# Gated attention and mixer block on one core: second-product tiles begin in any free strip, hand-over pause 0.51, first raw tokens loaded before their row statistics

## The chip, the cores and the metric

The kernel runs on one core of a Trainium2 chip. The core has a matrix engine (PE, with its weight loads as PEld), a vector engine (DVE), a scalar engine (ACT), GpSimd (POOL) and a queue engine (SP), each with an instruction queue of its own. They meet through semaphores. The metric is the time of one execution in device microseconds. Before the change it was 1044.77 us, the median of three runs between 1043.12 and 1045.74.

## What is computed

One input x of 2048 tokens by 448 features goes through two branches, and a gate per token mixes them. All operands are float32; the matrix products are made from high and low parts, three products for one.

```python
def reference(A_x, A_wqkv, A_wo, B_x, B_w1, B_b1, B_w2, B_b2, gate_w):
    x = A_x
    g = sigmoid((x * gate_w).sum(-1, keepdims=True))
    # A: 16 heads of 28: softmax(q k^T / sqrt(28)) v, then wo
    a = attention(x, A_wqkv, A_wo)
    # B: layernorm over features, 448 -> 1792, GELU (tanh form), 1792 -> 448
    y = (x - mean) / sqrt(var + 1e-5)
    b = gelu(y @ B_w1 + B_b1) @ B_w2 + B_b2
    return g * a + (1 - g) * b
```

## The kernel before

The work has two stages. In the **strip stage** the array is used as four strips of 32 rows. Each strip works off matmuls of its own, and four run side by side. A tile of output (128 x 512 or 128 x 448, in one of six PSUM banks, the buffer `bk`) needs a visit to each of the four strips; the kernel makes these one after the other, since all four add into the same bank. The tiles come in this order: queries and keys (`QK`, 25 tiles here, after three made with the whole array), values (`Val`, 16), then for each chunk c of 512 tokens 14 tiles of the first MLP product (`Up`, operands `w1f` and `yh`/`yl`) and 4 tiles of the second (`Down`, operands `w2h`/`w2l` and `hh`/`hl`). An Up, QK or Val tile takes 42 matmuls in its four visits, a Down tile 168, since its sum runs over all 14 hidden tiles. Up has 512 columns, Val and Down 448 or 450.

Beside them the strips make **row maxima** (line 212 on PE, line 214 on DVE): for each head the maximum over the keys of a 128 x 512 block of scores, needed by the softmax later. There are 1024 of them; 578 stand in the strip stage, and the rest in the attention stage, one or two in a turn (`lone`).

In the **attention stage** a loop of 257 turns makes scores (line 1139), exponentials on ACT (line 1145) and the products with the values (line 1183). An agenda puts DMAs and GpSimd work at given turns. In the last of the four head groups it also fetches the MLP result (`fetch_acc`, line 982), weighs it on GpSimd (`weigh_acc`, lines 986 and 987), and projects with wo (lines 1001 to 1003).

What sets the order: `Strips.run` is a planner that runs while the program is built. It holds a time for each strip, DVE, ACT, POOL and the DMAs, takes the strip that is free first, and gives it a matmul of a tile whose operands are ready by its own count. Otherwise it moves that strip on by 0.1. Its figures are numbers in the code: 0.232 for a matmul of 512 columns, 0.204 for one of Down, `HOP` for the pause between the end of a visit and the begin of the tile's next visit in another strip, and some for each helper. The result is a fixed order for every queue. At a hand-over, SP waits for the last matmul of a visit and raises the semaphore `hand` (line 529); the first matmul of the next visit waits for it (line 487).

A Down tile i begins in strip i and goes round from there (`next`, line 378). Its products stand in a fixed order: high parts of the hidden tile by both parts of w2 for f = 0 to 13, then the low parts. `lacks` (line 389) asks for the next product in that order only.

The layer norm: `want_stats` reads x and makes means and variances on DVE; `rows` turns them into two rows, stored to DRAM (line 142). `want_ln(c)` loads these rows for chunk c to all partitions (`lnr`, line 160) and the raw tokens of the chunk (`raw`, four tiles), subtracts the mean (line 679 on GpSimd for c > 1, line 686 on DVE otherwise), multiplies (line 691, GpSimd) and splits into `yh` (ACT, line 707) and `yl` (GpSimd, line 708). All of chunk c must be split before its first Up product.

Of the kernel before, what the change touches and what calls it, by code (L numbers as in the profile page):

```python
# [35 lines left out]
def kernel(ctx: ExitStack, tc: tile.TileContext, xt, wqk, wv, wo, xk, w1, b1, w2, b2,  # L36
# [204 lines left out]
    HOP = 0.6  # L241
# [5 lines left out]
    hh, hl = [], []  # L247
    mhp = []

    class Piece:  # L250
# [10 lines left out]
        def lacks(self, st, m, now):  # L261
            return False

# [105 lines left out]
    class Down(Piece):  # L369
# [3 lines left out]
        fixed = True  # L373

# [3 lines left out]
        def next(self, s):  # L378
            return s == (self.i + 4 - len(self.rem)) % 4
# [9 lines left out]
        def lacks(self, st, m, now):  # L389
            f, p = (m // 2, 0) if m < 2 * NF else (m - 2 * NF, 1)  # L390
            return st.hready.get((self.c, f, p), 1e9) > now or self.c == 0 and st.w2ready.get(f, 1e9) > now
# [12 lines left out]
    class Strips:  # L404
# [44 lines left out]
        def pick(self, s, now, over=None):  # L449
            for x in self.live:  # L450
                if x.bar(self):
                    continue
                if x.next(s) and not x.busy and x.ready <= now and (over is None or isinstance(x, Up) and x.c == over.c):
                    return x
            if over is None and self.tiles and self.tiles[0].next(s) and self.tiles[0].start(self, now):
                b = min(self.free, key=lambda b: self.free[b], default=None)
                if b is not None and self.free[b] <= now:
                    x = self.tiles.pop(0)
                    x.bank = b
                    del self.free[b]  # L460
                    self.live.append(x)
                    started(self, x, now)
                    return x
            return None

        def run(self):
            while self.tiles or self.live:
# [12 lines left out]
                if v is None or v[0].lacks(self, v[2], now):  # L480
                    self.t[s] = now + 0.1
                    continue
                x, ops, m = v
                a, b = ops[m] if not x.fixed else (ops[m][0][ops[m][2]][ops[m][3], ops[m][4]], ops[m][1][ops[m][2]][ops[m][3]])
# [173 lines left out]
    def rows(st):  # L658
        ln_std()
        st.use("dve", st.clock, 0.15)  # L660
        st.use("act", st.dve + 0.2, 2.2)

        def second():
            ln_rows()
            st.use("dve", st.clock, 0.6)
            st.at(st.dve + 0.2, ln_store)
            st.at(st.dve + 3.5, lambda: want_ln(st, 0))
            for f in range(NW, NF):
                st.at(st.dve + 3.6, lambda f=f: want_w1(st, f, kept=True))
            st.at(st.dve + 3.7, st.feed.pump)  # L670

        st.at(st.act + 0.2, second)

    def want_ln(st, c):
        cs = slice(c * CH, (c + 1) * CH)

        def use(t, r, late=False):
            if c > 1:
                nc.gpsimd.tensor_sub(r, r, lnr[c][:, 0])
                st.use("pool", st.clock, 1.35)  # L680
                scale(t, r)
                return
            if c == 0 and not late:
                st.at(st.clock + 1.5, lambda: use(t, r, True))
# [12 lines left out]
        for t in range(4):  # L697
            st.feed.add(xt[t, :, cs], 256, lambda r, t=t: use(t, r), kept=True,
                        first=(lambda: ln_rows_load(c)) if t == 0 else None)
# [88 lines left out]
    def schedule_head(st):  # L788
# [4 lines left out]
        st.late, st.later = False, []  # L793
# [8 lines left out]
        for f in range(NW):  # L802
            want_w1(st, f, after=54.0)
# [272 lines left out]
    def begun(n, turn):  # L1076

        g, c = divmod(n, NC)
        if n + 1 < NG * NC:
# [3 lines left out]
            at(turn + 10, lambda: load_ms(n + 1))  # L1083
# [7 lines left out]
        if g == NG - 1:  # L1091
            for i in range(TPC):
                at(turn + 8 + i, lambda i=i: fetch_acc(c, i))
                at(turn + 10 + i // 2, lambda i=i: weigh_acc(c, i))
# [3 lines left out]
    def valued(n, turn):  # L1098
# [9 lines left out]
        if g == NG - 1:  # L1108
            for i in range(TPC):
                tail.append((turn + 8 + i, c * TPC + i))  # L1110
# [153 lines left out]
```

## Time and profile before

| | us |
|---|---|
| runs | 1043.12, 1044.77, 1045.74 |
| profiled execution, own time | 1043.61 |
| its span (first to last instruction) | 1041.8 |
| before the strips (loads, first three QK tiles) | 0 to 16.6 |
| strip stage, first to last matmul of line 488 | 16.6 to 447.9 |
| attention stage, to the end of PE's work | 447.9 to 1036.6 |
| last DVE work, last stores, end of program | 1036.6 to 1041.8 |
| granted clock, mean | 0.999 |

The page's share of busy time counts PE as busy when any strip works. Four strips that are each busy, and one that is busy while three wait, look the same in it. How full the strips are is read from the number of matmuls that a stretch of time holds. A stretch also counts the ones that were already running when it began, so the short ones count some more per microsecond than the long ones, and a stretch is compared with a full one of the same kind and length.

### The profile page before, as it was taken

The page shows a single profiled execution, that of the slowest core. Times are in us where ns is not written, and L with a number is a line of the kernel's source. Part 1 is how long each engine was busy: PE and PEld are TensorE (multiplying, and loading weights), DVE is VectorE, ACT ScalarE, POOL GpSimd, SP SyncE. Part 2 cuts the span into 40 slices and gives each one's busy share as a digit, 9 for nine tenths or more (in the row PEclk, how much of TensorE's full clock was granted, in tenths as well). Part 3 has the DMA queues.
Part 4 walks back from the last instruction along what each step waited for, and adds up shares of the span by engine and source line. Part 5 has one row for each costly group of instructions (what it writes and reads, how often), then busy time and mean ns, then how long its engine had stood idle before and what let it go on. Part 6 is the DMA issues. An engine that isn't in the chain of part 4 may idle for free.

```text
span 1041.8 us, 30993 instructions
## 1 busy us (share of the span) xinstructions
PE 1033.5 (99%) x13170; PEld 683.0 (66%) x13170; DVE 748.6 (72%) x1182; ACT 663.3 (64%) x1016; POOL 369.1 (35%) x392
## 2 busy tenths in 40 slices
PE   9999999999999999999999999999999999999998
PEld 6999999999999999954444444444444444454455
DVE  4899898999999999966666666466666666634101
ACT  5334365044034034079999999999999999957763
POOL 5566468526325026651111011220111224463451
PEclk9999999999999999999999999999999999999999
DMA  7686533221210012350010101320002202111121
GB/s 242 208 257 217 205 110 98 72 66 30 61 38 12 7 43 55 82 155 23 14 26 22 30 5 40 82 60 13 20 21 65 53 12 57 30 64 48 53 66 45
DMA packets 47787, 73.20 MB, mean 70 GB/s; under 512 B 13840, under 2 KB 28816, under 8 KB 46848
## 3 DMA queue, kind: packets, MB, share of 16 engines
q1 hardware_dynamic: 33888, 39.11, 13.4%
q0 software_dynamic: 5120, 16.89, 5.8%
q10 hardware_dynamic: 8640, 15.21, 4.0%
q8 instruction: 103, 1.69, 0.7%
q14 instruction: 36, 0.29, 0.1%
HBM read 51.75 MB, written 19.31 MB: 68 GB/s over the span
## 4 chain that ended last, share of the span: by engine, by line
PE 99%; DMA 0%; DVE 0%; SPq 0%; issue 0%; ACT 0%
PE bk L488 37%; PE bk L1183 25%; PE bk L1139 17%; PE bk L212 15%; PE bk L1001 2%; PE bk L1003 1%; PE bk L1002 1%; PE bk L920 1%; DMA first<-in_xt 0%; PE bk L945 0%; PE bk L1066 0%; SPq L898 0%; PE bk L1060 0%; DVE xl L106 0%; DVE ob L1023 0%
## 5 line engine op out<-in xcount | busy, mean ns | idle before, releaser
L214 DVE TENSOR_REDUCE mx<-bk 128x1 f32<-128x512 f32 x1024 | 683.3, 689 | 185.0 <-PE bk L212 163.0
L1145 ACT ACTIVATE p<-bk 128x1024 f32<-128x1024 f32 x743 | 510.6, 760 | 64.5 <-PE bk L1139 39.4
L212 PE MATMUL bk<-kd,qd 28*128 28x512 f32 x1024 | 439.6, 430 | 0.0
L212 PEld LDWEIGHTS bk<-kd,qd 28*128 28x128 f32 x1024 | 186.1, 182 | 198.0 <-DVE mx L214 173.8
L488 PE MATMUL bk<-yh,w1f 32*128 32x512 f32 x1568 | 191.5, 393 | 0.0
L488 PE MATMUL bk<-yl,w1f 32*128 32x512 f32 x784 | 166.7, 392 | 0.0
L488 PEld LDWEIGHTS bk<-yh,w1f 32*128 32x128 f32 x1568 | 154.9, 183 | 1.2 <-ACT h L355 0.2
L488 PE MATMUL bk<-w2h,hh 32*128 32x448 f32 x896 | 145.3, 367 | 0.0
L488 PE MATMUL bk<-w2l,hh 32*128 32x448 f32 x896 | 144.2, 363 | 0.0
L1041 POOL TENSOR_TENSOR ot<-ob,rc 128x512 f32<-128x512 f32 x12 | 15.4, 1284 | 346.3 <-DMA rc<-rls 226.6
L1183 PE MATMUL bk<-p,vb 128*32 128x512 f32 x1024 | 136.6, 605 | 0.1
L1183 PE MATMUL bk<-p,va 128*32 128x512 f32 x1024 | 136.4, 605 | 0.0
L363 POOL TENSOR_TENSOR hl<-h,hh 128x512 fp32r<-128x512 f32 x56 | 72.5, 1308 | 132.9 <-ACT hh L356 106.7
L488 PEld LDWEIGHTS bk<-yl,w1f 32*128 32x128 f32 x784 | 106.0, 183 | 0.1
L488 PEld LDWEIGHTS bk<-w2h,hh 32*128 32x128 f32 x896 | 103.5, 183 | 0.4
L488 PEld LDWEIGHTS bk<-w2l,hh 32*128 32x128 f32 x896 | 103.5, 183 | 0.2
L488 PE MATMUL bk<-w2h,hl 32*128 32x448 f32 x896 | 93.1, 362 | 0.0
L1139 PE MATMUL bk<-yh,ka 29*128 29x512 f32 x512 | 92.5, 470 | 0.0
L1139 PE MATMUL bk<-yh,kb 29*128 29x512 f32 x512 | 87.6, 477 | 0.0
L398 ACT ACTIVATE gb<-bk 128x448 f32<-128x448 f32 x8 | 4.4, 545 | 129.4 <-PE bk L488 129.4
L355 ACT ACTIVATE h<-bk,b1s 128x512 f32<-128x512 f32 x56 | 38.3, 684 | 73.6 <-PE bk L488 67.4
L488 PEld LDWEIGHTS bk<-w2h,hl 32*128 32x128 f32 x896 | 82.1, 183 | 0.3
(141 smaller groups left out, 1637.2 us busy)
## 6 DMA issues: line engine op xcount, KB each, us to landing
qk<-qo ACTq DMA_DIRECT2D x28, 256.0 KB
raw<-in_xt SPq DMA_DIRECT2D x17, 256.0 KB
vs<-vt ACTq DMA_DIRECT2D x16, 256.0 KB
rc<-rls SPq DMA_DIRECT2D x60, 64.0 KB
bxr<-in_xk POOLq DMA_DIRECT2D x8, 448.0 KB, 6.3
acc<-gbs SPq DMA_DIRECT2D x16, 224.0 KB
out_y<-acc SPq DMA_DIRECT2D x16, 224.0 KB
qd<-qk SPq DMA_DIRECT2D x60, 56.0 KB
```

The lines of the kernel that those rows point to most:

```text
L212: nc.tensor.matmul(ps, self.qd[n % 2][r, i * P:(i + 1) * P], self.kd[r, k * 512:(k + 1) * 512], start=True, stop=True)
L214: nc.vector.reduce_max(self.mx[n % 2][:, j, i, k:k + 1], ps, axis=AX)
L355: nc.scalar.activation(h, bk[:, self.bank], AF.Gelu_apprx_tanh, bias=b1s[:, f:f + 1])
L363: nc.gpsimd.tensor_sub(hl[f], h, hh[f].bitcast(F32))
L488: mm = nc.tensor.matmul(bk[:, x.bank, :n], a, b, start=x.first, stop=(len(x.rem) == 1 and m == len(ops) - 1), skip_group_check=True)
L920: nc.tensor.matmul(bk[:, b], w, v, start=(i == 0), stop=(i == len(ops) - 1), skip_group_check=True)
L1001: nc.tensor.matmul(po, h, woh[:, g], start=(g == 0), stop=False, skip_group_check=True)
L1002: nc.tensor.matmul(po, h, wol[:, g], start=False, stop=False, skip_group_check=True)
L1041: nc.gpsimd.tensor_mul(ot[g][:, c * CH:(c + 1) * CH], ob, rc)
L1139: nc.tensor.matmul(bk[:, b], w[r, ks], q[r], start=(p == 0), stop=(p == 2), skip_group_check=True)
L1145: nc.scalar.activation(t[:, i:e], bk[:, b + i:b + e], AF.Exp, scale=SCALE)
L1183: nc.tensor.matmul(bk[32 * j:32 * j + 32, 7], vg[n // NC][:, k, 32 * j:32 * j + 32], prob[4 * b + j], start=(k == 0), stop=(k == NT - 1), ...
```

## The change

It touches six things.

1. `HOP` falls from 0.6 to 0.51. It moves instructions in the planner's order; no wait is taken out of the program.
2. A Down tile begins in any strip in which no other Down tile of its chunk began (`begun_in`), and goes round from there.
3. In a visit the planner takes the next product whose operands are ready, and not the next in the fixed order (the list is rearranged with `ops.insert(m, ops.pop(k))`). So low parts can come ahead of high parts. The sum is the same up to the order of additions.
4. The raw tokens of chunk 0 are asked for when the statistics are done, and the `lnr` load stands apart in `shift_rows`; the subtractions are held until the planner expects `lnr`. The first ten w1 tiles are asked for from 60 and not from 54 of the planner's time.
5. For chunk 1 the subtraction goes from DVE to GpSimd, as it did for chunks 2 and 3.
6. In the attention stage `load_ms` goes from turn + 10 to turn + 13, `fetch_acc` and `weigh_acc` move by 4 turns, the projections of chunk 1 move by 4 turns, `lone` prefers the strip with the most row maxima until the least has 192, and a strip's newly loaded keys count as there 2 turns sooner.

```diff
-    HOP = 0.6
+    HOP = 0.51
...
+    begun_in = set()
...
-        def lacks(self, st, m, now):
+        def lacks(self, st, op, now):
             return False
+
+        def begin(self, s):
+            pass
...
+        first_strip = None
...
         def next(self, s):
-            return s == (self.i + 4 - len(self.rem)) % 4
+            if self.first_strip is None:
+                return (self.c, s) not in begun_in
+            return s == (self.first_strip + 4 - len(self.rem)) % 4
+
+        def begin(self, s):
+            if self.first_strip is None:
+                self.first_strip = s
+                begun_in.add((self.c, s))
...
-        def lacks(self, st, m, now):
-            f, p = (m // 2, 0) if m < 2 * NF else (m - 2 * NF, 1)
+        def lacks(self, st, op, now):
+            f, p = op[2], int(op[0] is hl)
...
-                if v is None or v[0].lacks(self, v[2], now):
+                k = next((k for k in range(v[2], len(v[1])) if not v[0].lacks(self, v[1][k], now)), None) if v else None
+                if k is None:
                     self.t[s] = now + 0.1
                     continue
                 x, ops, m = v
+                ops.insert(m, ops.pop(k))
...
-            st.at(st.dve + 3.5, lambda: want_ln(st, 0))
+            st.at(st.dve + 3.5, shift_rows)
...
+        def shift_rows():
+            ln_rows_load(0)
+            st.use("pool", st.clock, 0.8)
+            st.shifted = st.get(st.pool, 512) + 0.7
+            for go in st.unshifted:
+                st.at(st.shifted, go)
+
         st.at(st.act + 0.2, second)
+        st.at(st.clock + 0.1, lambda: want_ln(st, 0))
...
-            if c > 1:
+            if c > 0:
                 nc.gpsimd.tensor_sub(r, r, lnr[c][:, 0])
...
-                st.at(st.clock + 1.5, lambda: use(t, r, True))
+                def go():
+                    use(t, r, True)
+
+                if st.shifted is None:
+                    st.unshifted.append(go)
+                else:
+                    st.at(max(st.clock, st.shifted), go)
...
-            want_w1(st, f, after=54.0)
+            want_w1(st, f, after=60.0)
...
-            at(turn + 10, lambda: load_ms(n + 1))
+            at(turn + 13, lambda: load_ms(n + 1))
...
-                at(turn + 8 + i, lambda i=i: fetch_acc(c, i))
-                at(turn + 10 + i // 2, lambda i=i: weigh_acc(c, i))
+                at(turn + 12 + i, lambda i=i: fetch_acc(c, i))
+                at(turn + 14 + i // 2, lambda i=i: weigh_acc(c, i))
...
-                tail.append((turn + 8 + i, c * TPC + i))
+                tail.append((turn + (12 if c == 1 else 8) + i, c * TPC + i))
...
-        s = min((s for s in strips if rowmax.ready(s) and turn >= cold[s]), key=lambda s: rowmax.cnt[s], default=None)
+        s = min((s for s in strips if rowmax.ready(s) and turn >= cold[s]), key=lambda s: rowmax.cnt[s] * (1 if min(rowmax.cnt) > 192 else -1), default=None)
...
-                cold[j] = turn + 7
+                cold[j] = turn + 5
```

Three places show what the planner makes of it. The numbers behind names are the program's own buffer numbers.

**GpSimd, at the end of the w1 splits of the strip stage**, before: the last w1 split, the load of the statistics rows, the four loads of raw tokens (`raw<-in_xt`), and the first multiplication and split of chunk 0.

```order
L97 TENSOR_TENSOR w1f9_2081<-raw0_130,w1f9_2081 64x128
L160 DMA lnr_2248<-lns_89 128x2x512
L571 DMA raw1_131<-in_xt 128x512
L571 DMA raw2_132<-in_xt 128x512
L571 DMA raw3_133<-in_xt 128x512
L571 DMA raw0_130<-in_xt 128x512
L691 TENSOR_TENSOR raw1_131<-raw1_131,lnr_2248 128x512
L708 TENSOR_TENSOR yl_111<-raw1_131,yh_110 128x512
```

The same place with the change:

```order
L160 DMA lnr_2008<-lns_89 128x2x512
L96 TENSOR_TENSOR w1f6_1934<-first1_135,w1f6_1934 128x384
L97 TENSOR_TENSOR w1f6_1934<-first1_135,w1f6_1934 64x128
L586 DMA raw2_132<-in_xt 128x512
L96 TENSOR_TENSOR w1f7_1964<-first2_136,w1f7_1964 128x384
L97 TENSOR_TENSOR w1f7_1964<-first2_136,w1f7_1964 64x128
L586 DMA raw3_133<-in_xt 128x512
L96 TENSOR_TENSOR w1f8_2106<-first3_137,w1f8_2106 128x384
L97 TENSOR_TENSOR w1f8_2106<-first3_137,w1f8_2106 64x128
L96 TENSOR_TENSOR w1f9_2140<-raw0_130,w1f9_2140 128x384
L97 TENSOR_TENSOR w1f9_2140<-raw0_130,w1f9_2140 64x128
L720 TENSOR_TENSOR raw1_131<-raw1_131,lnr_2008 128x512
```

The first raw load stands three rows ahead of this piece, and the fourth in the row right behind it. So three of the four now stand among the w1 splits, the first of them ahead of `lnr`; the fourth waits for its buffer `raw0`, which holds w1 tile 9 until that is split.

**PE, at the border of the Up and Down tiles of chunk 0**, before: `hh13` is the last hidden tile's high part, and `hl` are low parts.

```order
L488 MATMUL bk_115<-w2h13_3789,hh13_2923 128x448 x3
L488 MATMUL bk_115<-w2h5_3391,hh5_2915 128x448
L488 MATMUL bk_115<-w2l13_3790,hh13_2923 128x448 x2
L488 MATMUL bk_115<-w2l5_3392,hh5_2915 128x448
L488 MATMUL bk_115<-w2l13_3790,hh13_2923 128x448
L488 MATMUL bk_115<-w2h0_3143,hl0_2924 128x448 x2
L488 MATMUL bk_115<-w2h6_3486,hh6_2916 128x448
L488 MATMUL bk_115<-w2h0_3143,hl0_2924 128x448
L488 MATMUL bk_115<-w2h1_3180,hl1_2925 128x448 x2
L488 MATMUL bk_115<-w2l6_3487,hh6_2916 128x448
```

The same border with the change:

```order
L503 MATMUL bk_115<-yh_110,w1f13_3003 128x512
L503 MATMUL bk_115<-w2l9_3601,hh9_2943 128x448
L503 MATMUL bk_115<-w2l10_3709,hh10_2944 128x448
L503 MATMUL bk_115<-w2h7_3534,hh7_2941 128x448
L503 MATMUL bk_115<-w2h10_3708,hh10_2944 128x448
L503 MATMUL bk_115<-w2h6_3509,hh6_2940 128x448
L503 MATMUL bk_115<-w2h0_3171,hl0_2948 128x448
L503 MATMUL bk_115<-w2l7_3535,hh7_2941 128x448
L503 MATMUL bk_115<-w2l10_3709,hh10_2944 128x448
L503 MATMUL bk_115<-w2l6_3510,hh6_2940 128x448
L503 MATMUL bk_115<-w2h1_3213,hl1_2949 128x448
```

Before, no low part stands ahead of the last high part of its tile. Now the low parts `hl0` and `hl1` stand among high parts 6 to 10, and so ahead of `hh11` to `hh13` of their own tile.

**SP, at the end of the program**, before: the result of the MLP comes in by `acc<-gbs` (line 982), the output goes out by `out_y<-acc` (line 1009). These are the last rows.

```order
L1035 DMA rc_16365<-rls_92 32x512 x4
L982 DMA acc_16481<-gbs_90 128x448
L1009 DMA out_y<-acc_16065 128x448
L982 DMA acc_16519<-gbs_90 128x448
L1009 DMA out_y<-acc_16104 128x448
L982 DMA acc_16559<-gbs_90 128x448
L1009 DMA out_y<-acc_16145 128x448
L982 DMA acc_16597<-gbs_90 128x448
L1009 DMA out_y<-acc_16183 128x448
L1009 DMA out_y<-acc_16481 128x448
```

With the change (lines 1011 and 1038):

```order
L1064 DMA rc_16367<-rls_92 32x512 x4
L1038 DMA out_y<-acc_16150 128x448
L1038 DMA out_y<-acc_16187 128x448
L1038 DMA out_y<-acc_16227 128x448
L1038 DMA out_y<-acc_16265 128x448
L1011 DMA acc_16621<-gbs_90 128x448
L1011 DMA acc_16643<-gbs_90 128x448
L1011 DMA acc_16669<-gbs_90 128x448
L1011 DMA acc_16693<-gbs_90 128x448
L1038 DMA out_y<-acc_16621 128x448
```

The last four loads of the MLP result stood one by one between the stores of the chunk ahead. Now all four stand behind the last of these stores.

The number of row maxima in the strip stage, counted in the order as built, is 569 and was 578. The number of attention turns stays 257.

More of the change, by code (lines that the diff above doesn't have):

```diff
@@ L459, in pick @@
                     x.bank = b
+                    x.begin(s)
                     del self.free[b]
@@ L698, in want_ln @@
             st.feed.add(xt[t, :, cs], 256, lambda r, t=t: use(t, r), kept=True,
-                        first=(lambda: ln_rows_load(c)) if t == 0 else None)
+                        first=(lambda: ln_rows_load(c)) if t == 0 and c else None)
         st.feed.pump()
@@ L792, in schedule_head @@
         st.wready.update({0: 0.0, 3: 0.0, 4: 0.0})
-        st.late, st.later = False, []
+        st.late, st.later, st.shifted, st.unshifted = False, [], None, []
         st.xs, st.wvn, st.stats, st.lns, st.go, st.yn = {}, 0, 0, {}, {0}, {}
```

## The prediction

> **What bounds the kernel now.** I read the page first, then windows of the strip stage, then the waits.
>
> ```profile
> PE 1033.5 (99%) x13170; PEld 683.0 (66%) x13170; DVE 748.6 (72%) x1182; ACT 663.3 (64%) x1016; POOL 369.1 (35%) x392
> 16.60:447.90 431.30, 430.68 (x7342) 413.68 (x7341) 406.56 (x655) 140.65 (x250) 214.98 (x225) 1.00 0.33 99
> ```
>
> PE bounds it, but "99%" hides the strips: one running strip makes PE busy. The second row is the whole strip stage: 7342 matmuls in 431.3 us. How many would fit? Two stretches without a border between kinds of tiles, Up in the first and mostly Down in the second, long and short:
>
> ```profile
> 375.00:395.00 20.00, 20.00 (x341) 19.36 (x340) 19.76 (x31) 8.92 (x14) 8.94 (x7) 1.00 0.01 3
> 355.00:375.00 20.00, 20.00 (x374) 19.32 (x370) 19.65 (x33) 2.18 (x4) 0.00 (x0) 1.00 0.18 61
> 375.00:380.00 5.00, 5.00 (x92) 4.85 (x90) 4.99 (x9) 2.53 (x4) 2.55 (x2) 1.00 0.02 3
> 355.00:360.00 5.00, 5.00 (x103) 4.79 (x97) 4.95 (x9) 0.00 (x0) 0.00 (x0) 1.00 0.01 3
> ```
>
> Full is 341 (Up) to 374 (Down) in 20 us, 92 to 103 in 5 us. By the tile counts the stage holds 3980 matmuls of 512 columns (25 QK and 56 Up tiles of 42, 578 row maxima) and 3360 of 448 or 450 (16 Val of 42, 16 Down of 168). At 341/20 and, for the short ones, 103 less some 6 that overlap the edge in 5 us, that is 3980/17.05 + 3360/19.4 = 233 + 173 = 406 us. So about **25 us of the stage are strips without work**. Where the idle lies:
>
> ```profile
> 105.00:110.00 5.00, 4.38 (x84) 3.71 (x81) 4.97 (x9) 1.11 (x4) 0.00 (x0) 1.00 0.92 345
> 120.00:125.00 5.00, 5.00 (x71) 4.36 (x66) 4.78 (x8) 2.34 (x7) 4.57 (x6) 1.00 0.63 211
> 140.00:145.00 5.00, 5.00 (x76) 4.78 (x75) 4.88 (x9) 4.69 (x9) 4.79 (x4) 1.00 0.19 50
> 160.00:180.00 20.00, 20.00 (x323) 18.96 (x322) 17.82 (x27) 9.27 (x16) 16.06 (x13) 1.00 0.45 126
> 240.00:245.00 5.00, 5.00 (x74) 4.71 (x69) 4.98 (x9) 3.55 (x6) 2.42 (x2) 1.00 0.01 1
> 255.00:260.00 5.00, 5.00 (x84) 4.74 (x81) 4.97 (x8) 0.00 (x0) 2.86 (x3) 1.00 0.23 47
> 320.00:340.00 20.00, 20.00 (x322) 18.75 (x322) 19.76 (x33) 8.50 (x14) 11.59 (x10) 1.00 0.04 12
> 425.00:440.00 15.00, 15.00 (x266) 14.54 (x264) 14.88 (x24) 0.00 (x0) 10.51 (x11) 1.00 0.08 21
> ```
>
> Against full windows of the same kind (92 or 103 in 5 us, 358, halfway, in the mixed 20 us, 280 in 15) they lack 0.9, 1.1, 0.9, 2.0, 1.0, 0.9, 2.0 and 0.8 us: **9.6 us in eight holes**, nearly all where Up gives way to Down or Val to Up. The other 15 us are spread out.
>
> **The change part by part.** It removes no matmul. Whatever it gains must come out of those 25 us.
>
> *Down tiles in any strip, products as they are ready.* The last five holes (6.7 us) are the borders of Up and Down. In 320 to 340 ACT works 8.5 and GpSimd 11.6 of 20 us, so the hidden tiles aren't short; a strip stands idle because no tile may begin there, or waits for one product while another is there. That is what the edit gives. In 160 to 180 GpSimd works 16.1 of 20, so this one is partly short of data. I take two thirds of the 6.7: **4.5 us**, between 0 and 6.7.
>
> *Raw tokens first.*
>
> ```profile
> 99.23 0.73 POOL L160 DMA_DIRECT2D lnr<-lns  x1 [1.81 <-DMA lns<-mrt]
> 110.27 1.28 POOL L691 TENSOR_TENSOR raw<-raw,lnr 128x512 f32<-128x512 f32 x1 [8.17 <-DVE raw L686]
> 122.27 1.30 POOL L708 TENSOR_TENSOR yl<-raw,yh 128x512 fp32r<-128x512 f32 x1
> 109.50 0.68 DVE L686 TENSOR_TENSOR raw<-raw,lnr 128x512 f32<-128x512 f32 x1
> lnr<-lns POOLq DMA_DIRECT2D x4, 512.0 KB, 7.2
> raw<-in_xt POOLq DMA_DIRECT2D x5, 256.0 KB, 7.0
> ```
>
> GpSimd stands idle for 8.2 us, and chunk 0 is split at 123.6. With three raw tiles there early, the first subtraction can follow `lnr`, at 99.2 + 7.2 = 106.4 and not 109.5; then come four multiplications and four splits at 1.3, with some DMA issues at 0.6: 106.4 + 0.7 + 10.4 + 1.2 = 118.7, so 4.9 us sooner. The fourth token is loaded later than the rest; at 7.0 us it costs up to 2 of these. Up products then fill the hole at 120 and help the one at 140, 2.0 us together; I take **1.6**. What is late next is the w1 splits, now behind these loads, but only tiles 10 to 13 come after chunk 0.
>
> *The pause of 0.51.* The program makes 339 hand-overs:
>
> ```profile
> L529 SPq EVENT_SEMAPHORE  x339: 17/17/17, 19.2 to 437.3; - x170
> SPq L529 <- PE bk L488: 312.7, 256, 9.4
> PEld bk L488 <- issue: 1.0, 1, 1.0
> L488 PE MATMUL bk<-yh,w1f 32*128 32x512 f32 x1568 | 191.5, 393 | 0.0
> L488 PEld LDWEIGHTS bk<-yh,w1f 32*128 32x128 f32 x1568 | 154.9, 183 | 1.2 <-ACT h L355 0.2
> ```
>
> At most it gains 339 x 0.09 / 4 = 7.6 us, if each time the strip had nothing else; at least 0. All pauses together are 339 x 0.6 / 4 = 51 us of four strips, and idle outside the holes is 15, so about 0.3 of them show: 0.3 x 7.6 = 2.3. In the holes it counts in full. I take **3.8**, half of the most. Is 0.51 enough? From the start of a visit's last matmul the planner leaves 0.232 + 0.51 = 0.742 us. Needed are 0.393 for the matmul, 0.017 for SP and 0.183 for the next weights: 0.593, and twice the way of a semaphore, which no row shows; 0.149 is left for it. SP is there in time: in 256 of the 339 it was SP that waited for PE. And the idle of PE's weight loads in the stage that is put down to nothing else is 1.0 us, once.
>
> What a late one costs:
>
> ```profile
> 43.96 0.18 PEld L488 LDWEIGHTS bk<-xl,wq 32*128 32x128 f32 x1
> 44.19 0.18 PEld L212 LDWEIGHTS bk<-kd,qd 28*128 28x128 f32 x1
> 44.19 0.18 PEld L488 LDWEIGHTS bk<-xl,wq 32*128 32x128 f32 x1
> 44.20 0.41 PEld L488 LDWEIGHTS bk<-xh,wq 32*128 32x128 f32 x5
> ```
>
> No weights for 0.23 us, then loads for several tiles within 0.01: what stands first in PE's queue holds what stands behind it, in all strips. So a hand-over that is late by t costs t, and not t/4.
>
> [...]
>
> *The subtraction on GpSimd* (chunk 1): four of 1.28 us more there, four of 0.7 less on DVE, which in the stage works 406.6 of 431.3 us. The first waits for its `lnr`, 7.2 us after the issue; behind it stand the multiplications and splits of chunk 1, and Up of chunk 1 waits for these. Down of chunk 0 hides that: it is worked on all the while. I put it at 0; if the cover fails, it is 4 x 1.28 = 5.1 less 4 x 0.7, 2.3 us late, once.
>
> *Nine row maxima fewer in the strips* (578 to 569) save 9/17.05 = 0.5 there. They go to turns of the attention stage:
>
> ```profile
> 469.73 1.00 PE bk L1183 x8
> 473.98 1.00 PE bk L1183 x8
> 984.22 1.01 PE bk L1183 x8
> 988.27 1.00 PE bk L1183 x8
> ```
>
> Two turns take 4.25 us with row maxima and 4.05 without, 0.1 a turn. Nine more in pairs are 4.5 turns: 0.5 us. The two cancel.
>
> *The end.* The last four weighings on GpSimd now follow the last store of the chunk ahead:
>
> ```profile
> 1012.26 0.38 SPq L982 DMA_DIRECT2D acc<-gbs  x1
> 1015.08 1.15 POOL L986 TENSOR_TENSOR acc<-acc,b2b 128x448 f32<-128x448 f32 x1 [1.92 <-DMA acc<-gbs]
> 1016.32 1.41 POOL L987 TENSOR_SCALAR acc<-acc,ngate 128x448 f32<-128x448 f32 x1
> 1015.68 0.68 DVE L1008 SCALAR_TENSOR_TENSOR acc<-bk,gate,acc 128x448 f32<-128x448 f32 x1 [3.88 <-PE bk L1003]
> 1033.17 1.72 POOL L1071 TENSOR_TENSOR ol<-ob,oh 128x128 fp32r<-128x128 f32 x4 [15.45 <-ACT oh L1070]
> ```
>
> In these times: store at 1016.4 + 0.4, four loads issued by 1018.5, the first landed 2.8 us after its issue (1012.26 to 1015.08), at 1019.6; then 4 x 2.6 = 10.4: GpSimd is free at 1030.0, and is wanted at 1033.2. The cover is 3.2 us of the 15.45 it idles there. Cost 0; every microsecond beyond the 3.2 is one at the end. `load_ms` is moved past three turns of SP's other loads and has 3 turns (6.4 us) left before its use, for a small load: 0. The new choice of `lone` changes which strip gets a row maximum, not how many a turn holds; newly loaded keys have 4 turns, 8.5 us, and where they come later PE waits by the difference: 0.
>
> *Cost.* With the pause nearer to what is needed, some hand-overs will hold PE, and with products taken as soon as the planner counts them ready, some will wait for ACT or GpSimd: I allow **0.6 us**, between 0 and 3.
>
> Sum: -4.5 - 1.6 - 3.8 + 0.6 = **-9.3 us**. The profiled execution took 1043.6 (span 1041.8 and 1.8 around it), so 1034.3; it lies 1.2 below the median shown, and from the median it would be 1035.5. I forecast **1034.5**, between the two. From the bounds: gains of 6.7 + 2.0 + 7.6 = 16 at most, and near 3 at the least that I believe.
>
> **The rivals.** *Hand-overs hold the whole array* (slower). If a hand-over needs on average 0.03 us more than it is given, 339 x 0.03 = 10 us eat the gain; at 0.045 it is 15.3, less the gains of 9.9, +5.4: **1049**. For it speaks only that 0.149 for two semaphore ways is not seen; against it, that 1.0 us at a pause of 0.6. Chance 0.05.
>
> *The holes are short of data.* Then an idle strip that may begin a tile finds no product ready, and only the pause and the raw tokens gain, at their low values, less the cost: 2.3 + 1.0 - 0.6 = 2.7, **1041.5** with the same allowance for the runs. For it: GpSimd's 16.1 of 20 at 160. Against: 11.6 at 320 and 2.4 of 5 at 240. Chance 0.08.
>
> *Half of it*: waits at some hand-overs and the late fourth token leave about half, 4.6 us: **1039.5**. Chance 0.13. *The end is uncovered*, loads landing 3 us later: +2 on the forecast, inside its range.
>
> **How the numbers follow.** Forecast 0.74 (own range 1031 to 1037.5), half 0.13, short of data 0.08, slower 0.05. A measurement of this kernel tells about 0.3% (3.1 us) from no change, so faster is 0.74 + 0.13 + 0.01, same 0.07, slower 0.05. The range takes in the forecast's and part of the half case: 1030.5 to 1039.5.
>
> **What would show it.** Right: the first attention product near 443 and not 452.6; the windows at the borders near 92 and 103; the first Up product of chunk 0 about 4 us sooner; PE's waits in the stage still near 1 us; turns of 2.13 us. Wrong: matmul counts of the stretches without a border falling below 341 and 374 (hand-overs hold PE), holes as deep as before beside an idle GpSimd, or GpSimd's last splits waiting for its own weighing.

## The result, and the profile after

| | before | changed |
|---|---|---|
| median, us (4 runs each, same chip; of before, the three shown above and one more) | 1044.64 | 1035.4 |
| lowest to highest | 1043.12 to 1045.74 | 1034.85 to 1037.8 |
| profiled execution, own time; span | 1043.61; 1041.8 | 1034.85; 1033.1 |
| granted clock, mean | 0.999 | 0.998 |

The ratio is 0.9917, with a 95% interval of 0.99 to 0.9934. The forecast was 1034.5 in a range of 1030.5 to 1039.5. Three executions of the experiments further down (one of the kernel before, one of e5 and one of e8) ran at a mean granted clock of 0.56 to 0.85 and took 1105 us or more; they are left out of medians and ratios, and e5, whose profile is of that execution, has no stage in the table.

The windows of the changed kernel, with the columns of the prediction's rows, named in the first line (the stretch, its length, then each engine's busy time with its number of instructions): first the whole strip stage, then the eight holes. The stage now ends 10 us sooner, so the last hole is sought at 415 to 430. The last row is a stretch that was no hole before.

```profile
core 0: us, PE busy (x) PEld busy (x) DVE busy (x) ACT busy (x) POOL busy (x), PEclk, DMA share, GB/s
17.30:438.20 420.90, 420.25 (x7332) 406.36 (x7331) 400.77 (x642) 139.35 (x248) 219.35 (x229) 1.00 0.34 102
105.00:110.00 5.00, 5.00 (x103) 5.00 (x100) 5.00 (x8) 2.40 (x8) 4.42 (x4) 1.00 0.37 126
120.00:125.00 5.00, 5.00 (x99) 4.83 (x95) 4.94 (x9) 1.21 (x4) 0.00 (x0) 1.00 0.48 158
140.00:145.00 5.00, 5.00 (x88) 4.96 (x84) 4.76 (x8) 4.09 (x8) 5.00 (x5) 1.00 0.29 90
160.00:180.00 20.00, 20.00 (x355) 19.56 (x355) 18.48 (x28) 9.38 (x16) 19.08 (x16) 1.00 0.41 125
240.00:245.00 5.00, 5.00 (x90) 4.84 (x86) 4.98 (x9) 2.64 (x4) 1.84 (x2) 1.00 0.01 3
255.00:260.00 5.00, 5.00 (x104) 4.64 (x100) 4.81 (x9) 0.00 (x0) 0.00 (x0) 1.00 0.92 249
320.00:340.00 20.00, 20.00 (x372) 19.30 (x369) 19.63 (x33) 5.94 (x10) 8.97 (x8) 1.00 0.02 6
415.00:430.00 15.00, 15.00 (x269) 14.44 (x266) 14.84 (x23) 0.00 (x0) 11.79 (x12) 1.00 0.22 51
115.00:120.00 5.00, 4.35 (x82) 4.31 (x85) 5.00 (x9) 1.24 (x3) 4.18 (x5) 1.00 0.52 172
```

The stage takes 420.9 and not 431.3 us, 10.4 less for nearly the same matmuls. At the places where they were, six of the eight holes are filled or nearly so: 120 to 125 holds 99 matmuls where it held 71, 240 to 245 90 for 74, 320 to 340 372 for 322. The one at 140 is better (88 for 76), the last is as it was (269 for 266). A new one stands at 115 to 120, with 82; there PE itself is idle for 0.65 us.

Of the 10.4 us, 8.8 reach the span (1041.82 to 1033.06): the stage began 0.7 later (17.3 for 16.6; kernels with the same beginning began it between 16.4 and 20.5 in other executions), the way from the start of its last matmul to the first attention product took 0.8 longer, and the attention stage, first to last product, took 573.6 us where it took 573.5. The 0.8 belongs to the new order: the way is 5.83 us here, 5.84 in a second trace of this kernel and 5.04 before. PE's weight loads now wait there for ACT, which still empties the last tiles' banks; before, no such wait stands at this place. By the waits from 437 to 446, and the first attention products by the view of line 1212:

```profile
PEld bk L1168 <- ACT gb L410: 0.9, 2, 0.5
...
L1212 PE MATMUL bk<-p,va x24: 592/604/617, 443.8 to 448.5; 128*32 128x512 f32 x24
```

443.8 stands against 452.6 before, and near 443 was forecast. The other signs came too: the first Up product of chunk 0 starts at 120.4 and not 124.6, the stretch of Up from 375 to 395 holds 345 matmuls where it held 341, and a turn of the attention stage takes 2.13 us.

The last split of chunk 0 ends at 117.44 + 1.30 = 118.74, as forecast (118.7; before 123.57). The rows of GpSimd and DVE around it (timeline of the changed kernel: start, duration, engine, line) show what made the new hole:

```profile
111.32 0.58 POOL L586 DMA_DIRECT2D raw<-in_w  x1
111.92 2.54 POOL L737 TENSOR_TENSOR yl<-raw,yh 128x512 fp32r<-128x512 f32 x2
115.10 1.28 POOL L720 TENSOR_TENSOR raw<-raw,lnr 128x512 f32<-128x512 f32 x1 [0.64 <-DVE raw L715]
...
117.44 1.30 POOL L737 TENSOR_TENSOR yl<-raw,yh 128x512 fp32r<-128x512 f32 x1
...
104.43 0.68 DVE L715 TENSOR_TENSOR raw<-raw,lnr 128x512 f32<-128x512 f32 x1
...
105.63 1.40 DVE L715 TENSOR_TENSOR raw<-raw,lnr 128x512 f32<-128x512 f32 x1
...
108.15 0.80 DVE L715 TENSOR_TENSOR raw<-raw,lnr 128x512 f32<-128x512 f32 x1
...
112.63 2.39 DVE L715 TENSOR_TENSOR raw<-raw,lnr 128x512 f32<-128x512 f32 x1
```

Four equal subtractions take 0.68, 1.40, 0.80 and 2.39 us. The long one ends at 115.02, 0.56 after GpSimd's two splits that run without a gap from 111.92 to 114.46. This is called a lockout below. Row maxima on DVE stand behind it, and PE waited for them. PE's waits between 20 and 440 (engine and tile, line, releaser; total, times, longest):

```profile
PEld bk L212 <- DVE mx L214: 1.4, 2, 1.0
PE bk L212 <- DVE mx L214: 0.6, 1, 0.6
...
PEld bk L503 <- SPq L544: 0.3, 1, 0.3
```

The last row is the hand-overs: 0.3 us, once. The 1.0 us of the first row is the one near 115. At the end of the program GpSimd finished its last weighing at 1020.27 + 1.40 = 1021.67 and waited 2.72 us, for ACT:

```profile
1020.27 1.40 POOL L1016 TENSOR_SCALAR acc<-acc,ngate 128x448 f32<-128x448 f32 x1
1024.40 1.72 POOL L1100 TENSOR_TENSOR ol<-ob,oh 128x128 fp32r<-128x128 f32 x4 [2.72 <-ACT oh L1099]
```

### The profile page after: what moved, and what is told of

It is laid out like the page before. It is cut to its first block, busy times and chain, and to the rows that moved or that the text cites. A ratio compares the mean times of both kernels' runs of the same rounds, so it can differ in the third digit from the quotient of the medians.

```text
span 1033.1 us, 30973 instructions
## 1 busy us (share of the span) xinstructions
PE 1024.8 (99%) x13170; PEld 676.9 (66%) x13170; DVE 749.2 (73%) x1178; ACT 662.9 (64%) x1018; POOL 372.9 (36%) x396
## 3 DMA queue, kind: packets, MB, share of 16 engines
q1 hardware_dynamic: 33888, 39.11, 13.5%
## 4 chain that ended last, share of the span: by engine, by line
PE 98%; DMA 1%; DVE 0%; ACT 0%; SPq 0%; issue 0%; ACTq 0%; DVEq 0%
PE bk L503 36%; PE bk L1212 25%; PE bk L1168 17%; PE bk L212 16%; PE bk L1030 2%; PE bk L1032 1%; PE bk L1031 1%; PE bk L949 1%; DMA first<-in_xt 1%; DVE raw L715 0%; PE bk L974 0%; DVE mx L214 0%; ACT gb L410 0%; PE bk L1095 0%; SPq L927 0%
## 5 line engine op out<-in xcount | busy, mean ns | idle before, releaser
L503 PE MATMUL bk<-yh,w1f 32*128 32x512 f32 x1568 | 186.4, 391 | 0.0
L503 PE MATMUL bk<-yl,w1f 32*128 32x512 f32 x784 | 161.8, 390 | 0.0
L503 PEld LDWEIGHTS bk<-yh,w1f 32*128 32x128 f32 x1568 | 151.1, 183 | 0.7 <-ACT gb L410 0.2
L503 PE MATMUL bk<-w2h,hl 32*128 32x448 f32 x896 | 88.8, 362 | 0.0
L1168 PE MATMUL bk<-yh,la 28*128 28x512 f32 x512 | 80.3, 393 | 0.0
L1168 PE MATMUL bk<-yl,ka 28*128 28x512 f32 x512 | 79.7, 390 | 0.0
```

The source lines that it names most:

```text
L503: mm = nc.tensor.matmul(bk[:, x.bank, :n], a, b, start=x.first, stop=(len(x.rem) == 1 and m == len(ops) - 1), skip_group_check=True)
L1168: nc.tensor.matmul(bk[:, b], w[r, ks], q[r], start=(p == 0), stop=(p == 2), skip_group_check=True)
```

## The experiments

Two theories. **A**: the terms of the prediction add up; each edit gains its own part wherever it stands. **B**: each edit makes the planner build another order for all that follows, and the time follows the clock that the planner itself reaches, not the sum of the edits. That clock (its time at the last matmul of the strip stage, in the same microseconds as `HOP`) can be read when the program is built: 427.9 for the kernel before, 417.2 for the changed one.

All kernels in one table. "Stage" is the trace's time from the start of the first to the start of the last matmul of the strips; ratios are to the kernel before on the same chip. "Difference" is the stage less the planner's clock.

| kernel | planner | stage | difference | median | ratio [95%] |
|---|---|---|---|---|---|
| before | 427.9 | 431.0 | 3.1 | 1044.64 | 1 |
| changed | 417.2 | 420.6 | 3.4 | 1035.4 | 0.9917 [0.99, 0.9934] |
| changed, again (e9) | 417.2 | 420.8 | 3.6 | 1034.2 | 0.9907 [0.9892, 0.9922] |
| e1 attention edits alone | 427.9 | 431.0 | 3.1 | 1043.88 | 1.0 [0.999, 1.0009] |
| e2 and the pause 0.51 | 428.0 | 430.1 | 2.1 | 1042.71 | 0.9991 [0.9981, 1.0] |
| e3 raw tokens late | 428.3 | 433.6 | 5.3 | 1046.11 | 1.0022 [1.0013, 1.0032] |
| e4 pause 0.6 | 423.8 | 427.3 | 3.5 | 1040.54 | 0.9971 [0.9958, 0.9984] |
| e6 fixed start strip | 424.5 | 428.3 | 3.8 | 1040.77 | 0.998 [0.9971, 0.9989] |
| e7 both Down edits undone | 421.4 | 424.7 | 3.3 | 1037.13 | 0.9944 [0.993, 0.9957] |
| e8 pause 0.30 | 415.8 | 423.2 | 7.4 | 1035.95 | 0.9927 [0.9909, 0.9945] |
| e5 one split moved | 417.2 | – | – | 1033.71 | 0.9915 [0.9901, 0.993] |
| e10 the same, again | 417.2 | 419.7 | 2.5 | 1033.11 | 0.9897 [0.9882, 0.9911] |
| e11 pause 0.55 | 422.6 | 429.4 | 6.8 | 1043.27 | 0.9997 [0.9988, 1.0007] |
| e12 late signals | 417.2 | 457.7 | 40.5 | 1071.5 | 1.0264 [1.0248, 1.0279] |

### e1 and e2: the attention edits alone, and with the pause

The kernel before with part 6 of the change (e1); then with the pause as well (e2, its edit beside e1's):

```diff
-    HOP = 0.6
+    HOP = 0.51
```

> The kernel before with the attention-stage edits alone (load of the maxima, fetch and weighing of the MLP result, projections of chunk 1, choice of the strip for a row maximum, keys ready sooner). The order of the strip stage is the one of before. Both theories: no difference, 1044.6 within 0.3%; the span from the first to the last product with the values stays at 573.0 us. If these edits carry part of the change, it shows here as 1 us or more.

> As e1, and the pause 0.51 for 0.6. Theory A (the terms of the prediction add up, each edit gains its own part): the pause gains 3.8 us, 1040.8. Theory B (the parts don't add; the time follows the time at which the planner itself puts the last matmul of the strips, which is 427.9 for before and 417.2 for the change): the planner puts it at 428.0, so no gain, 1044.7.

The attention edits alone do nothing, as the prediction had it. The pause gains 0.9 us with them, at most 2.0 by the interval, and not the 3.8 of the prediction: with the fixed rules for Down the planner fills no hole with it (428.0 for 427.9).

### e3 and e4: the changed kernel, one part undone

In e3 part 4 of the change is undone (shortened):

```diff
-            st.at(st.dve + 3.5, shift_rows)
+            st.at(st.dve + 3.5, lambda: want_ln(st, 0))
...
-            want_w1(st, f, after=60.0)
+            want_w1(st, f, after=54.0)
```

> The change, with the raw tokens of chunk 0 asked for late and w1 from 54, as before; the pause, the Down tiles and the subtraction of chunk 1 as in the change. Theory A: 1.6 us of the gain go, 1037.0. Theory B: the planner puts the last strip matmul at 428.3, so the whole gain goes, 1046. The first product of Up of chunk 0 is about 5 us later than in the change in both.

In e4 the pause goes back:

```diff
-    HOP = 0.51
+    HOP = 0.6
```

> The change with the pause at 0.6. Theory A: 3.8 us of the gain go, 1039.2. Theory B: the planner puts the last strip matmul at 423.8, 6.6 later than with 0.51, so 1042.0. Row maxima in the strip stage 579 for 569.

With the raw tokens late, all of the gain is gone, and 0.2% more: 0.0105 of the time, 11 us, for a part put at 1.6. Where they went, by windows of e3, then of the changed kernel:

```profile
170.00:175.00 5.00, 5.00 (x85) 4.55 (x80) 4.81 (x8) 3.37 (x6) 4.92 (x5) 1.00 0.13 48
175.00:180.00 5.00, 4.15 (x20) 1.57 (x17) 5.00 (x9) 0.63 (x1) 4.92 (x5) 1.00 0.00 0
180.00:185.00 5.00, 5.00 (x46) 4.81 (x50) 3.73 (x6) 0.63 (x1) 4.92 (x5) 0.50 0.11 31
185.00:190.00 5.00, 5.00 (x86) 4.76 (x83) 3.71 (x7) 0.00 (x0) 1.70 (x2) 0.82 0.89 268
```

```profile
175.00:180.00 5.00, 5.00 (x103) 4.92 (x102) 5.00 (x9) 1.26 (x2) 4.84 (x5) 1.00 0.01 3
180.00:185.00 5.00, 5.00 (x95) 4.97 (x91) 4.97 (x8) 0.63 (x1) 4.92 (x5) 1.00 0.04 11
```

The strips of e3 hold 20 matmuls in 5 us and not 103; between 167 and 190 their time without work is some 7 us more than in the changed kernel, the lowered clock (next to last column but one: 0.50) included. GpSimd's timeline there, of e3 (its lines: 701 subtraction, 713 multiplication, 367 low parts of the hidden tiles, 730 low-part split), then of the changed kernel:

```profile
170.77 1.29 POOL L701 TENSOR_TENSOR raw<-raw,lnr 128x512 f32<-128x512 f32 x1
172.14 1.29 POOL L713 TENSOR_TENSOR raw<-raw,lnr 128x512 f32<-128x512 f32 x1
173.39 1.29 POOL L367 TENSOR_TENSOR hl<-h,hh 128x512 fp32r<-128x512 f32 x1
174.63 1.29 POOL L701 TENSOR_TENSOR raw<-raw,lnr 128x512 f32<-128x512 f32 x1
176.00 1.27 POOL L713 TENSOR_TENSOR raw<-raw,lnr 128x512 f32<-128x512 f32 x1
177.24 1.26 POOL L367 TENSOR_TENSOR hl<-h,hh 128x512 fp32r<-128x512 f32 x1
```

```profile
168.40 2.93 POOL L367 TENSOR_TENSOR hl<-h,hh 128x512 fp32r<-128x512 f32 x2 [0.66 <-ACT hh L360]
171.29 1.29 POOL L702 TENSOR_TENSOR raw<-raw,lnr 128x512 f32<-128x512 f32 x1
```

In the kernel before, which also asks for the raw tokens late but subtracts on DVE, the last two low parts came ahead of chunk 1's first operation on GpSimd:

```profile
170.94 2.55 POOL L363 TENSOR_TENSOR hl<-h,hh 128x512 fp32r<-128x512 f32 x2 [1.42 <-ACT hh L356]
175.21 1.29 POOL L691 TENSOR_TENSOR raw<-raw,lnr 128x512 f32<-128x512 f32 x1 [1.73 <-DVE raw L686]
```

In e3 the last two low parts of chunk 0 stand behind subtractions and multiplications of chunk 1 and end at 174.7 and 178.5; in the changed kernel both are done at 171.3, before chunk 1 begins. From 174.2 to 180.8 PE in e3 starts only products of low parts that have just come, and row maxima. So the cover failed of a term that the prediction put at nothing, the subtraction of chunk 1 on GpSimd. No run has the changed kernel with this subtraction back on DVE, so its share in the 11 us is argued from these rows. And it cost a second time: behind the thin stretch the granted clock is 0.50 from 180 to 185 and 0.82 for the next five. That is 2.5 + 0.9 us at most, and of the size of the 2 us by which e3 exceeds its planner's clock more than the others do. PE was not idle ahead of it: busy for 4.15 of the 5 us, with 20 matmuls. What lowers the clock is not shown by these rows.

The pause of 0.6 loses 5.6 us (0.9917 to 0.9971) where A has 3.8 and B 6.6. With some 2 us of uncertainty, this run alone doesn't tell them apart.

### e6 and e7: the two Down edits

The fixed start strip again; in e7 with the fixed order of products too.

```diff
-            if self.first_strip is None:
-                return (self.c, s) not in begun_in
-            return s == (self.first_strip + 4 - len(self.rem)) % 4
+            return s == (self.i + 4 - len(self.rem)) % 4
...
-                k = next((k for k in range(v[2], len(v[1])) if not v[0].lacks(self, v[1][k], now)), None) if v else None
+                k = v[2] if v and not v[0].lacks(self, v[1][v[2]], now) else None
```

> The changed kernel with one part undone: a Down tile i of a chunk begins in strip i again; products are still taken as they are ready. Theory A (each edit gains its own part): some of the 4.5 us of the two Down edits are lost, 1036 to 1040. Theory B (time follows the order that the planner happens to build; its own clock has the last matmul of the strip stage at 424.5 for this kernel, 417.2 for the changed one, 427.9 for the kernel before): 7.3 later than the changed kernel by the planner, 1042.7, more than undoing both Down edits together.

> The changed kernel with both Down edits undone: a Down tile i begins in strip i, and its products come in the fixed order. Theory A: 4.5 us later than the changed kernel, 1039.9, and the windows at the borders of Up and Down are as thin as before the change. Theory B: the planner's own clock has the last matmul of the strip stage at 421.4, 4.2 later than the changed kernel: 1039.6, and 3.1 sooner than with the fixed start strip alone. This run alone does not tell the theories apart; with the one on the fixed strip it does.

Undoing one Down edit costs 0.0063, 6.6 us, where B has 7.3; undoing both costs 0.0027, 2.8 us, where A has 4.5 and B 4.2. The intervals of e6 and e7 are apart, so no split in which each Down edit gains something can be right. A split in which products as they are ready lose 3.8 us by themselves would fit these two runs; no run undoes that edit alone. The pause settles that edits don't add: it gains 0.9 in e2 and its undoing costs 5.6 in e4, with intervals that are apart. The planner's clock has e6 and e7 in this order.

The other sign of A, borders as thin as before, fails in e7:

```profile
160.00:180.00 20.00, 20.00 (x342) 19.41 (x340) 18.81 (x28) 9.55 (x17) 19.11 (x17) 1.00 0.42 126
240.00:245.00 5.00, 5.00 (x81) 4.82 (x82) 5.00 (x9) 2.59 (x4) 2.56 (x2) 1.00 0.00 0
320.00:340.00 20.00, 20.00 (x365) 19.48 (x361) 19.81 (x33) 8.33 (x14) 11.43 (x9) 1.00 0.04 9
```

These held 323, 74 and 322 matmuls before, and 355, 90 and 372 with all edits. By the count of the table further down, 3.9 of the 6.1 us that the borders gained are there without either Down edit.

### e11 and e8: a little more pause, and far less

In the changed kernel `HOP` is 0.55 (e11) and 0.30 (e8, where `load_ms` also goes to turn + 14).

> The changed kernel with the planner's pause at 0.55. Theory A (the pause gains in proportion: 0.09 were put at 3.8 us): 0.04 longer is 1.7 us later, 1037. Theory B (time follows the order that the planner builds): its clock has the last matmul of the strip stage at 422.6, 5.4 later than the changed kernel: 1040.5, nearly all that the pause of 0.6 lost.

> The changed kernel with the planner's pause at 0.30 (and the reload of the row statistics in the attention stage one turn later, which costs nothing). The planner's clock has the last matmul of the strip stage at 415.8, 1.4 sooner than the changed kernel. From the start of a visit's last matmul the planner then leaves 0.53 us; the hand-overs that are used at once took about 0.67 us in the changed kernel. If a late hand-over held only its own strip, a quarter of it would show: about 1034 to 1036. If it holds the whole array, every hand-over that the order uses at once is 0.14 us late at the full price: with 45 to 100 such hand-overs 6 to 14 us, less the 1.4, so 1040 to 1048, and the waits of PE's weight loads for SP in the strip stage, 0.3 us in the changed kernel, rise to several us.

A pause of 0.55 loses the whole gain, more than 0.6 does. In proportion it would be 1.7 us; by the planner 5.4; against e9, run beside it, 9.1 were measured. What the planner doesn't have is in part in the trace: a hand-over that was late for a reason of its own (waits of e11 from 66 to 73, then SP's timeline there).

```profile
PEld bk L503 <- issue: 1.9, 1, 1.9
...
PE bk L503 <- SPq L544: 1.5, 1, 1.5
...
SPq L196 <- DMA qk<-qo: 1.8, 1, 1.8
```

```profile
69.36 0.31 SPq L196 DMA_DIRECT2D qd<-qk  x1
70.38 0.68 SPq L839 DMA_DIRECT2D sel<-in_sel  x1
71.17 0.54 SPq L840 DMA_DIRECT2D ident<-in_ident  x1
```

SP stood 1.8 us at a load that waited for a store, then issued `sel`, and the signal (it came at 71.10, between `sel` and `ident`) stood behind both. PE had no weights for 1.9 us. The stage is 3.2 us longer against its planner than e9's (6.8 for 3.6); 1.9 are this one, 0.4 a wait for DVE near 115 that is 1.4 us and not 1.0, and the rest isn't located.

At 0.30 the planner gains 1.4 and the kernel loses some 1 to 2 us by the ratios, whose intervals overlap; the stage, 423.2 for 420.6, is 4.0 us longer against its planner than the changed kernel's. The same lockout of DVE as above is longer here (2.92 us for 2.39), so some 3.5 are left: less than the 6 to 14 of a hold of the whole array. Not all of it is hand-overs. PE's weight loads between 20 and 440:

```profile
PEld bk L503 <- SPq L544: 1.6, 5, 0.4
PEld bk L212 <- DVE mx L214: 1.2, 1, 1.2
PEld bk L503 <- ACT h L359: 0.9, 3, 0.4
PEld bk L503 <- POOL hl L367: 0.4, 1, 0.4
```

The hand-overs' waits rose from 0.3 to 1.6 us, not to the several that were expected of a hold of the whole array; another 1.3 are waits for ACT and GpSimd, 0.4 in the changed kernel.

### e12: signals late by a known time

```diff
-                sig = nc.sync.sem_inc(hand, 1)
+                for k in range(8):
+                    sig = nc.sync.sem_inc(spent, 1)
+                    if k == 0:
+                        tc.add_manual_dep(sig.ins, mm.ins.name, handoff, reason="handoff")
+                sig = nc.sync.sem_inc(hand, 1)
```

> The changed kernel with eight increments of a semaphore that nothing waits for between the end of each visit and its signal on SP. At 17 ns each the 339 signals come about 0.14 us later; no other engine's order changes. By the slack of each hand-over in the changed kernel 88 of the 339 would then come too late, by 8.1 us in all. If a late hand-over costs its whole delay (the price that the prediction used): 8 us, so 1043. If it costs its own strip alone, a quarter: 2 us, 1037. If PE has enough loaded weights to run past so short a hold: below 1 us, 1035 to 1036.

All three numbers were wrong, since the dose was: increments follow each other on SP at 0.06 us (the first of eight at 20.3, the signal behind them at 20.8), not 0.017, and the signals came 0.47 us later (median of the 339), not 0.14. The waits of e12, whole program:

```profile
PEld bk L504 <- SPq L549: 35.9, 85, 1.3
```

PE's weight loads stood still for 35.9 us at 85 late signals, about as much as the kernel lost.

With the dose as measured, each of the 339 hand-overs can be worked through: its time of signal and of use in the changed kernel, what the holds ahead have already moved, and the queue on SP. The author's estimate from these times is about 58.6 us if a late one costs its whole delay, and 15.9 at a quarter. Measured: 457.7 for 420.8, 36.9 us. An estimate with the first 0.15 us of each hold at nothing and the rest at its full length gives 37.8; the 0.15 is fitted to e12, no other run tests it, and no row shows a cause for it. What is measured is a loss of about six tenths of the first estimate, neither all of it nor a quarter.

### e5 and e10: one lockout taken away

On GpSimd, chunk 0's third split is put behind the fourth multiplication. Nothing else moves. (The lines that define `low`, which holds this split back, are left out.)

```diff
-                    lambda: nc.gpsimd.tensor_sub(yl[:, t], r, yh[:, t].bitcast(F32)), "pool", 1.35,
+                    low, "pool", 1.35,
```

> The changed kernel with one instruction moved: of chunk 0's twelve layer-norm operations on GpSimd, the third low-part split now stands behind the fourth multiplication and not ahead of it. Nothing else moves on any engine. In the changed kernel DVE's fourth subtraction of chunk 0 lasts 2.39 us (others 0.68 to 1.40) and ends 0.55 us after the second of two GpSimd operations that run back to back beside it, and PE then waits 1.0 us for DVE's row maximum. Theory L (a DVE operation with two SBUF operands and a GpSimd operation shut each other out): the fourth subtraction ends about 1.2 us sooner, PE's wait of 1.0 us at that place is gone, chunk 0's last split stays within 0.2 us of 118.74, and the time falls by 0.5 to 1.0 us against the changed kernel: 1034.4 to 1034.9. Theory M (the subtraction was long because its operand or its slot came late): its length and PE's wait stay, and the time is that of the changed kernel, 1035.4.

> The changed kernel as it is, on the same chip as the three runs beside it: 1035 (1034 to 1036), first attention product near 443.8, DVE's fourth subtraction of chunk 0 2.39 us long. It is the base for the other three.

> The same kernel as in the run with the third split of chunk 0 moved behind the fourth multiplication. Theory L (a DVE operation with two SBUF operands and a GpSimd operation shut each other out): DVE's fourth subtraction lasts at most 1.4 us and not 2.39, PE's wait for DVE's row maximum falls from 1.4 to 0.4 us or less, the strip stage is 1.0 us shorter against its order, and the time is 0.5 to 1.0 below the changed kernel of this batch. Theory M (the operand came late): no difference.

The first of the two, e5, had no changed kernel beside it; e10 has e9. DVE and GpSimd in e10:

```profile
112.47 1.17 DVE L715 TENSOR_TENSOR raw<-raw,lnr 128x512 f32<-128x512 f32 x1
...
111.78 1.30 POOL L739 TENSOR_TENSOR yl<-raw,yh 128x512 fp32r<-128x512 f32 x1
113.72 1.29 POOL L720 TENSOR_TENSOR raw<-raw,lnr 128x512 f32<-128x512 f32 x1 [0.64 <-DVE raw L715]
```

With one GpSimd operation beside it and not two, the subtraction ends 0.56 after that one, at 113.64: 1.17 us long. PE's wait for DVE near 115 is gone (it was 1.0 us in the changed kernel, 0.9 in e9), the stage is 1.1 us shorter than e9's, and the median 1.1 lower (1033.11 for 1034.2). The ratios' intervals overlap, so the time alone doesn't settle the size; the rows do. Theory M falls. This is the fastest kernel of the study.

## Why the prediction was right, and where it was not

*The total and its place* were right. The stage's time without work was put at 25 us; counted as below it was 31.8. The 25 rests on 17.05 and 19.4 matmuls a microsecond, from stretches that were not quite full; four strips that each repeat a matmul at the times given below make 17.4 and 19.7. Before and after, counted as strip time without work in slices of 10 us (each matmul's start weighed with a quarter of 0.2295 or 0.2035 us, the author's estimate of the time after which a strip repeats a matmul of 512 or of 448 to 450 columns; in the changed kernel's trace the fourth start after a matmul lies 0.232 or 0.204 us behind it, by the median, where all are of one width):

| stretch of the stage | before | changed |
|---|---|---|
| 107 to 157 (chunk 0 begins) | 6.0 | 3.1 |
| 157 to 187, 237 to 267, 287 to 347 (borders) | 12.3 | 6.2 |
| all the rest | 13.5 | 12.6 |

So 2.9, 6.1 and 0.9 us went, 9.9 in all, and 0.5 for nine row maxima fewer: the 10.4 of the stage. The three gains of the prediction were 1.6, 4.5 and 3.8, 9.9 as well; but those stand ahead of its cost of 0.6, and the measured ones have the waits of the stage in them.

*The pause*, put at -3.8, half of the most, with a part "spread out": mis-sized, or rather not a size of its own. The stretches without a hole gained 0.9 with all edits together, with the attention edits alone the edit gains 0.9, and undone in the changed kernel it costs 5.6. What it is worth shows only with the other edits, and the times over the pause (0.30, 0.51, 0.55, 0.6: 0.9927, 0.9907, 0.9997, 0.9971) are not even in order. "Half of the most" priced an input of a planner as though it were a wait in the program.

*Raw tokens first*, -1.6: its mechanism was right to 0.1 us (118.7), and the hole at 120 is filled. What the term left out is that the early chunk 0 is what covers the subtraction on GpSimd: without it, in e3, the low parts of chunk 0 fall behind chunk 1, and 11 us go. *The subtraction*, put at 0 because "Down of chunk 0 hides that", or at 2.3 if it didn't: hidden in the changed kernel, which has no gap there (103 and 95 matmuls at 175 and 180), but with GpSimd at 19.08 of 20 us; where the cover failed, in e3, the price was some 7 us, the lowered clock included. What is late there is not only the next chunk's split but the operands of the work that was to be the cover.

*Down tiles*, -4.5: the borders gave 6.1 with all edits together, and undoing both edits costs 2.8 to 3.9 (against the two batches of the changed kernel). Counted as in the table, e7's borders hold 8.4 us without work, so of the 6.1 some 2.2 need the Down edits and 3.9 are there without them. As a whole the term is somewhat too large, and e6 shows that it can't be divided into two gains. The rival of holes short of data falls: with 372 matmuls in 320 to 340 they were not.

*Row maxima, the attention stage, the end*: as predicted. Nine row maxima left the strips; e1's ratio is 1.0, and the cover of the last weighings was 2.72 us where 3.2 was forecast.

*The cost*, 0.6 in a range of 0 to 3: wrong in place. It was put at hand-overs and products not yet ready. Hand-overs waited 0.3 us. What it cost stands elsewhere, where no term had it: 1.0 us for DVE shut out by GpSimd, near 115, and 0.8 for ACT at the passage to the attention stage.

*The price of a late hand-over*, t and not t/4: too high, by e12: for a median delay of 0.47 about six tenths of the sum, 36.9 us where 58.6 were estimated at t. The quarter, which the prediction set against it, is too low: 15.9. The slower rival fell because hand-overs at 0.51 weren't late: 0.3 us of waits.

So the sum came out right by luck in its parts. By place, the pause's 3.8 was too large by 2.9, and the two groups of holes too small by 1.3 and 1.6. By edit there is no such account: undone one at a time, raw tokens, pause and Down edits cost 11, 5.6 and 2.8 us, 19 in all, of a gain of 9. That the gain lay in the holes, which were read from the profile, held; how it was shared among the edits did not.

## What to carry to other kernels

Where a list scheduler writes the order, read the change's worth from the whole order that it builds and from the holes that it can fill, not edit by edit: parts neither add nor act in proportion, and a small step of one number can lose all of the gain. The scheduler's own clock is a good guide here (the stage lies 2.1 to 3.8 us above it in nine of the twelve rows that have a stage and leave the signals alone), and where the trace departs further, part of the departure was found at one place: a queue shared by signals and loads (1.9 us in e11), a lockout of two engines (a subtraction of 2.92 us in e8, and of 0.68 alone), a lowered clock (0.50 and 0.82 for 5 us each in e3). When work is moved onto an engine behind a cover, ask what that engine makes for the cover itself.

## What the hardware showed that was not expected

- DVE's four subtractions of chunk 0, with two operands in SBUF, took in the changed kernel 0.68 us without a GpSimd operation beside them, 0.80 and 1.40 beside one, of which 0.25 and 0.85 us were left, and 2.39 beside two that follow without a gap; the last three ended 0.55 to 0.56 after GpSimd's. It can be GpSimd that is late instead: in the kernel before, DVE's fourth subtraction (114.17, 0.84 us) ended 0.55 after the first of two GpSimd operations without a gap, and the second (114.43) took 1.74 us, where chunk 0's others took 1.27 to 1.30. DVE's row maxima, which read one operand from PSUM, took 0.69 us on average throughout. What the two SBUF operands have to do with it, no run tells apart.
- In e3, five microseconds with 20 matmuls in place of 103 were followed by a granted clock of 0.50 over the next five.
- Increments of a semaphore on SP, 17 ns long in their rows, followed each other only every 0.06 us in e12.
